# Order and form of the first loads, place of the filter copies, and number of product buffers in a fused spectral filter and feed-forward kernel

## The chip, the cores and the metric

The kernel runs on one core of a Trainium2 chip. The time is the device time of one launch in microseconds, the median of three runs. A core has TensorE (PE, matmul; PEld is its weight load), VectorE (DVE), ScalarE (ACT), GpSimd (POOL) and SyncE (SP), which works on queues of DMA transfers. Data lie in SBUF (128 partitions), matmul results in PSUM (8 banks), inputs and outputs in device memory.

## What is computed

```python
def _attn_ref(x, filt_r, filt_i):              # x: 8 x 3008 x 256 fp32
    X = np.fft.rfft(x, axis=1)                 # along the 3008 rows
    Y = X * (filt_r + 1j * filt_i)[None]       # a filter for each frequency and column
    return np.fft.irfft(Y, n=x.shape[1], axis=1).astype(np.float32)

def _moe_ref(x, w_in, w_out):                  # x: 24064 x 256, d_ff = 2048
    h = x @ w_in
    return (np.maximum(0.01 * h, h) @ w_out).astype(np.float32)
```

The second function takes the result of the first. The eight batches go through both, one after the other.

## The kernel before

The transform of 3008 = 94 x 32 is four stages of matmuls in fp16. Stage 1 (`s1`) transforms over 94 rows with `fwd1`, stage 2 (`s2`) over 32 with 24 matrices `f2_sb`, then the product with the filter, stage a (`sa`) and stage b (`sb`) go back. The result `yt` goes through the feed-forward part in 47 chunks of 512 tokens.

Between the stages the data have to change their place among the partitions. For the first batch VectorE does this with transposes (`t1`, `t2`), since nothing else is ready to run; batches 1 to 7 do it through device memory (`dz1`, `dz2`), beside the feed-forward part of the batch before. So the time falls into two parts: the first batch alone (its order of steps is the string `FIRST`), and everything after, in which TensorE does the feed-forward part with the later batches' stages between.

The loads at the start. GpSimd's queue casts fp32 to fp16 on the way; SyncE's queue [...] carries the constant matrices, which are fp16:

```python
    nc.sync.dma_start(small_sb[:], small_d.ap())               # fwd1, inv2 and others
    for i in (1, 0):
        nc.sync.dma_start(f2_sb[:, ts(i, NC // FP), :], f2_d.ap()[i])   # two thirds of stage 2's matrices
    first_parts = ((0, 10), (10, 10), (20, 8), (28, 4))
    for n0, nn in first_parts:
        x_load(0, n0, nn)                                      # batch 0, by GpSimd
    for hf in range(2):
        filt_load(0, filt_r, hf * DH, DH)                      # half of the columns; two transfers each
        filt_load(64, filt_i, hf * DH, DH)
        if hf == 0:
            nc.gpsimd.dma_start(f2_sb[:, ts(2, NC // FP), :], f2_d.ap()[2])
    nc.gpsimd.dma_start(w_in_sb[:], moe_w_in.rearrange("(dt p) c -> p dt c", p=P))
```

The steps of the first batch. `p` fills a PSUM bank, `e` empties it on ScalarE (A) or VectorE (D). `s2d` multiplies with the filter on VectorE straight out of PSUM; `s2a` copies to SBUF on ScalarE, and `s2m` multiplies there on GpSimd[...]. `warm` is matmuls on a tile of zeros whose result nobody uses:

```python
    spare = [scrp.tile([P, 4, DH], FP32, tag=f"p{i // 2 + 1}", name=f"spare{i}") for i in range(6)]

    def keep_warm(n):
        for _ in range(n):
            nc.tensor.matmul(po_ps..., idle[:, 0:P], idle[:], start=True, stop=True)
    def s1p(_, n0, n, b):                      # rows n0 to n0 + n into bank b
        ...
            nc.tensor.matmul(ps[:, ds(j, 2), :], fwd1[:N1], x_sb[:N1, ds(n0 + j, 2), :], start=True, stop=True)
    def s1e(_, n0, n, e):
        spread(big[0], n0, held.pop(("s1", n0)), engine[e])
    def t1(i):                                 # a quarter of the transposes after stage 1; t2 after stage a
        ...
        nc.vector.transpose(o[:, ts(i, E4)], a)
    def s2p(hf, c, n, i, b):                   # half hf of the columns, matrices c to c + n, part i, bank b
        ...
    def load_i1():                             # stage b's matrices
        nc.vector.memset(i1_sb[:, 0, 0:2], 0.0)
        nc.sync.dma_start(i1_sb[:], i1_d.ap())
    def load_x():                              # batch 1, and the output weights
        x_load(1, 0, N2 // 2)
        nc.gpsimd.dma_start(w_out_sb[:], moe_w_out.rearrange("(ct p) d -> p ct d", p=P))
        x_load(1, N2 // 2, N2 // 2)
```

Batches 1 to 7 take the product like this. Two buffers each of `p1`, `p2`, `p3`; the halves of `p2` change places by DMA (or, for every second group of batch 1, VectorE writes them in their new places):

```python
    scrp = ctx.enter_context(tc.tile_pool(name="scr", bufs=2))
    def s2_group(b, g):
        ...
            p1, p2, p3 = (scrp.tile([P, 2, D], FP32, tag=f"p{i}", ...) for i in (1, 2, 3))
            if b == 1 and g % 2 == EXG:
                nc.vector.tensor_tensor(p3[0:64], ps[64:P], fb[64:P], AL.mult)
                nc.vector.tensor_tensor(p3[64:P], ps[0:64], fb[0:64], AL.mult)
            else:
                nc.vector.tensor_tensor(p2[:], ps, fb, AL.mult)
                soon(AFTER[1], lambda: nc.sync.dma_start(p3[0:64], p2[64:P]))
                soon(AFTER[1], lambda: nc.sync.dma_start(p3[64:P], p2[0:64]))
            nc.vector.tensor_tensor(p1[:], ps, fa, AL.mult)
            ...  # later, on GpSimd: y1 = p1 + p3
```

For this they need the filter in another layout than the first batch, and VectorE makes it in six copies. `at(t, f)` puts `f` at a place `t` in the order in which instructions are issued; eight units are one chunk of the feed-forward part:

```python
    TWICE = (1.43, 1.84)
    for i in range(2):
        k1s = ts(i, NC // 2)
        for n, f in enumerate((
                lambda v=k1s: nc.vector.tensor_scalar(fb_sb[64:P, v], fa_sb[64:P, v], -1.0, None, AL.mult),
                lambda v=k1s: dve(fb_sb[0:64, v], fa_sb[64:P, v]),
                lambda v=k1s: dve(fa_sb[64:P, v], fa_sb[0:64, v]))):
            at(TWICE[0] + TWICE[1] * (3 * i + n), f)
```

Of the kernel before, what the change touches and what calls it, by code (L numbers as in the profile page):

```python
# [11 lines left out]
P = 128  # L12
FP16 = mybir.dt.float16
FP32 = mybir.dt.float32
# [5 lines left out]
N1, N2 = 94, 32  # L20
NC = 24
Q = 32
R1 = 96
FP = 3
# [51 lines left out]
def kernel(  # L76
# [9 lines left out]
    nc = tc.nc  # L86
    B, N, D = x.shape
# [16 lines left out]
    SUMS = (0.09, 1.59, 2.35, 4)  # L104
    REST = (5.37, 14.61, 8.86, 10.48, 23.53, 20.72)
    DUE = (3.52, 0.66)
    TWICE = (1.43, 1.84)
    F2T = 3.24
    LEAD = (3.85, 7.37)
    AFTER = (0.53, 0.8, 1.33, 3.17, 0.39, 0.52)  # L110
# [10 lines left out]
    f2_d = nc.inline_tensor(f2_np, name="fwd2_const")  # L121
    i1_d = nc.inline_tensor(i1_np, name="inv1_const")
# [5 lines left out]
    f2_sb = cpool.tile([P, NC, P], FP16, name="f2_sb")  # L128
    i1_sb = cpool.tile([P, N2, N1], FP16, name="i1_sb")
# [4 lines left out]
    w_out_sb = cpool.tile([P, NCT, D], FP16, name="w_out_sb")  # L134
    wt_sb = cpool.tile([P, 4, NCH, P], FP16, name="wt_sb")
    x_sb = cpool.tile([P, N2, D], FP16, name="x_sb")
    big = [cpool.tile([P, Q * D], FP16, name=f"big{i}") for i in range(3)]
# [1 line left out]

    gtp = ctx.enter_context(tc.tile_pool(name="gtp", bufs=2))  # L140
    drp = ctx.enter_context(tc.tile_pool(name="drp", bufs=1, space=bass.MemoryType.DRAM))
    scrp = ctx.enter_context(tc.tile_pool(name="scr", bufs=2))
    ypp = ctx.enter_context(tc.tile_pool(name="ypp", bufs=4))
    outp = ctx.enter_context(tc.tile_pool(name="outst", bufs=4))
    psp = ctx.enter_context(tc.tile_pool(name="psp", bufs=1, space=bass.MemoryType.PSUM))
# [18 lines left out]
    def at(time, f):  # L164
        clock["n"] += 1
        heapq.heappush(work, (time, clock["n"], f))
# [8 lines left out]
    def noted(what, f):  # L175
        f()
        issued.add(what)
# [10 lines left out]
    def x_load(b, n0=0, nn=N2, d0=0, dn=D):  # L188

        for lo, cnt in ((0, R1),) if b + 1 < B else ((0, 64), (64, N1 - 64)):  # L190
            nc.gpsimd.dma_start(
                x_sb[lo : lo + cnt, ds(n0, nn), ds(d0, dn)],
                bass.AP(tensor=x.tensor, offset=x.offset + (b * N + lo * N2 + n0) * D + d0,
                        ap=[[N2 * D, cnt], [D, nn], [1, dn]]))

    def filt_load(lo, src, d0, dn):

        for q, first, sgn in ((lo, 0, 1), (lo + Q, N1, -1)):
            nc.gpsimd.dma_start(
                fa_sb[q : q + Q, :, ds(d0, dn)],  # L200
                bass.AP(tensor=src.tensor, offset=src.offset + first * D + d0,
                        ap=[[N1 * D, N2 // 2], [sgn * NC * D, 2], [sgn * D, NC], [1, dn]]))


    nc.sync.dma_start(small_sb[:], small_d.ap())
    for i in (1, 0):
        nc.sync.dma_start(f2_sb[:, ts(i, NC // FP), :], f2_d.ap()[i])
    first_parts = ((0, 10), (10, 10), (20, 8), (28, 4))
    for n0, nn in first_parts:
        x_load(0, n0, nn)  # L210
    for hf in range(2):

        filt_load(0, filt_r, hf * DH, DH)
        filt_load(64, filt_i, hf * DH, DH)
        if hf == 0:
            nc.gpsimd.dma_start(f2_sb[:, ts(2, NC // FP), :], f2_d.ap()[2])
    nc.gpsimd.dma_start(w_in_sb[:], moe_w_in.rearrange("(dt p) c -> p dt c", p=P))
    idle = cpool.tile([P, CH], FP16, name="idle")
    nc.vector.memset(idle[:], 0.0)
# [136 lines left out]
    engine = {"A": act, "D": dve}  # L356
# [87 lines left out]
        sb_matmuls(ps, dt, h)  # L444
        quad_copy(h, dt, ps, copy)

    def load_i1():
        nc.vector.memset(i1_sb[:, 0, 0:2], 0.0)
        nc.sync.dma_start(i1_sb[:], i1_d.ap())

    def load_x():

        x_load(1, 0, N2 // 2)
        nc.gpsimd.dma_start(w_out_sb[:], moe_w_out.rearrange("(ct p) d -> p ct d", p=P))
        x_load(1, N2 // 2, N2 // 2)
        issued.add(("x", 1, 0))

    FIRST = """
        warm 18, s1p 0 0 2 b0, s1e 0 0 2 A, s1p 0 2 4 b3, s1p 0 6 4 b4, s1e 0 2 4 D, warm 4, s1p 0 16 4 b3,
        s1e 0 16 4 D, s1p 0 10 2 b1, s1e 0 6 4 A, s1p 0 12 4 b4, s1e 0 10 2 A, warm 2, s1p 0 24 2 b2,  # L460
        s1e 0 12 4 A, s1e 0 24 2 D, s1p 0 20 4 b3, s1e 0 20 4 A, s1p 0 26 2 b0, s1p 0 28 2 b1,
        s1p 0 30 2 b2, s1e 0 26 2 D, s1e 0 28 2 A, s1e 0 30 2 D, t1 1, t1 0, warm 14, s2p 0 0 4 0 b0,
        s2p 0 0 4 1 b1, s2p 0 16 4 0 b2, t1 2, t1 3, s2a 0 0 4 0, s2m 0 0 4 0, s2a 0 0 4 1, s2p 0 16 4 1 b0,
        s2p 0 8 8 0 b4, s2p 0 8 8 1 b3, s2a 0 16 4 0, s2m 0 16 4 0, s2a 0 16 4 1, s2m 0 16 4 1,
        s2p 0 4 4 0 b1, s2d 0 8 8 0, s2p 0 20 4 1 b2, s2d 0 8 8 1, i1, s2d 0 4 4 0, s2p 0 4 4 1 b0,
        s2p 1 8 8 0 b4, s2d 0 4 4 1, warm 1, s2p 1 8 8 1 b3, s2a 1 8 8 0, s2m 0 0 4 1, sap 0 8 b1,
        s2a 1 12 8 0, s2p 1 16 8 0 b4, s2d 0 20 4 1, sap 0 16 b0, s2m 1 12 8 0, x, s2a 1 8 8 1, s2m 1 8 8 1,
        s2d 1 16 8 0, sae 0 8 A, s2a 1 12 8 1, sae 0 16 A, s2p 0 20 4 0 b2, sap 0 4 b1, s2m 1 12 8 1,
        s2p 1 16 8 1 b3, sap 0 0 b0, s2p 1 0 8 1 b4, s2d 0 20 4 0, s2d 1 16 8 1, sae 0 4 A, s2m 1 8 8 0,
        sae 0 0 A, sap 0 20 b1, s2d 1 0 8 1, sap 0 12 b2, s2p 1 0 8 0 b3, sap 1 16 b0, sae 0 20 A,  # L470
        sae 0 12 A, sap 1 12 b1, s2d 1 0 8 0, sap 1 20 b2, t2 0, sap 1 8 b4, t2 1, sae 1 16 A, sap 1 4 b0,
        sap 1 0 b3, sae 1 12 A, warm 5, sbp 0 1 b1, sae 1 20 A, sae 1 8 A, sbp 0 4 b2, sae 1 4 A, sae 1 0 A,
        t2 3, sbp 0 5 b4, sbe 0 1 A, sbp 0 2 b0, t2 2, sbe 0 4 A, sbp 0 6 b3, sbe 0 5 A, sbp 0 7 b1,
        sbp 0 0 b2, sbp 0 3 b4, sbe 0 6 A, sbp 1 1 b3, sbe 0 0 D, sbe 0 2 A, sbp 1 0 b0, sbe 0 3 A,
        sbe 0 7 A, sbe 1 1 D, sbe 1 0 A
    """
    steps = dict(s1p=s1p, s1e=s1e, t1=t1, s2p=s2p, s2d=s2d, s2a=s2a, s2m=s2m, sap=sap, sae=sae, t2=t2,
                 sbp=sbp, sbe=sbe, i1=load_i1, x=load_x, warm=keep_warm)
    for step in FIRST.split(","):
        what, *args = step.split()  # L480
        steps[what](*(int(v) if v.isdigit() else v for v in args))
# [175 lines left out]
# [7 lines that stand above are left out]
    at(F2T, lambda: noted(("f2t",), lambda: nc.sync.dma_start(f2_sb[:], f2t_d.ap())))  # L664
    at(26, lambda: noted(("i1t",), lambda: nc.sync.dma_start(i1_sb[:K4], i1t_d.ap())))
    for b in range(1, B):
        z = 47 * (b - 4) if b > 4 else 0
        p = PLANS[min(b, 4) - 1]
# [18 lines left out]
    while queue:  # L687
        time, n, stage, b, g, f = heapq.heappop(queue)
# [62 lines left out]
```

## Time and profile before

| What | Value |
| --- | --- |
| time, median of 3 | 753.74 us (753.54 to 753.84) |
| span of the profiled run | 752.2 us |
| granted TensorE clock | 0.999 |
| busy: PE, DVE, ACT, POOL | 738.8, 499.3, 559.0, 163.6 us |
| first matmul of stage 1 | 8.02 us |
| VectorE's transposes after stage 1 | start at 14.68 us |
| first matmul of the feed-forward part | 36.23 us |

A line of the groups or the timeline of the profile names the line of the kernel, the engine, the operation, what it writes and reads, and how long it took; "[0.96 <-PE ph L388]" behind it says that the engine stood idle for 0.96 us before, and that the bank written at line 388 by TensorE released it. A line of the waits gives the engine that waited, for whom, the sum in microseconds, how often and the longest. Lines of the kernel before that matter here: 250 is stage 1 of batches 1 to 7 and 253 its copy out of PSUM, 299 stage 2, 308 and 311 the products, 314 GpSimd's sum, 321 stage a, 342 stage b, 379 and 425 the transposes of the first batch, 388 and 392 its stage 2, 396 its products, 406 and 419 ScalarE's copies, 502 the first matmul of the feed-forward part.

### The profile page before, as it was taken

The page shows a single profiled execution, that of the slowest core. Times are in us where ns is not written, and L with a number is a line of the kernel's source. Part 1 is how long each engine was busy: PE and PEld are TensorE (multiplying, and loading weights), DVE is VectorE, ACT ScalarE, POOL GpSimd, SP SyncE. Part 2 cuts the span into 40 slices and gives each one's busy share as a digit, 9 for nine tenths or more (in the row PEclk, how much of TensorE's full clock was granted, in tenths as well). Part 3 has the DMA queues.
Part 4 walks back from the last instruction along what each step waited for, and adds up shares of the span by engine and source line. Part 5 has one row for each costly group of instructions (what it writes and reads, how often), then busy time and mean ns, then how long its engine had stood idle before and what let it go on. Part 6 is the DMA issues. An engine that isn't in the chain of part 4 may idle for free.

```text
span 752.2 us, 19384 instructions
## 1 busy us (share of the span) xinstructions
PE 738.8 (98%) x8016; PEld 528.9 (70%) x8016; DVE 499.3 (66%) x683; ACT 559.0 (74%) x755; POOL 163.6 (22%) x169
## 2 busy tenths in 40 slices
PE   8999999999999999999999999999999999999997
PEld 3655667767777777877778777787777777777775
DVE  5886645777767776666676656776677576465565
ACT  3775797888878777787777787787777777777662
POOL 5503330342322311221133222212212210000000
PEclk9999999999999999999999999999999999999999
DMA  9986788887876557655676566544554333111011
GB/s 191 229 217 158 180 201 245 203 190 192 233 192 162 142 171 213 137 150 152 183 190 167 143 170 169 150 129 128 144 154 122 106 107 104 52 54 54 29 52 62
DMA packets 119688, 113.34 MB, mean 151 GB/s; under 512 B 16352, under 2 KB 92768, under 8 KB 119408
## 3 DMA queue, kind: packets, MB, share of 16 engines
q1 hardware_dynamic: 104447, 95.36, 42.7%
q0 software_dynamic: 14864, 16.49, 16.0%
q8 instruction: 62, 1.02, 0.6%
q10 hardware_dynamic: 289, 0.26, 0.1%
q14 instruction: 26, 0.21, 0.1%
HBM read 57.51 MB, written 50.33 MB: 143 GB/s over the span
## 4 chain that ended last, share of the span: by engine, by line
PE 91%; DMA 2%; DVE 2%; POOL 1%; ACT 0%; issue 0%; SPq 0%; DVEq 0%; ACTq 0%
PE ph L502 42%; PE po_ps L566 18%; PE pf L566 18%; PE pf L250 3%; PE pf L342 3%; PE pf L321 2%; PE pf L299 2%; PE po_ps L627 1%; PE pf L627 1%; DMA dz<-big 1%; DMA p_b_g<-p_b_g 1%; POOL prod L396 0%; DMA big<-dz 0%; POOL y_b_g L314 0%; DVE big L425 0%
## 5 line engine op out<-in xcount | busy, mean ns | idle before, releaser
L507 ACT ACTIVATE gt_c<-ph 128x1024 f16<-128x1024 f32 x376 | 385.4, 1025 | 134.8 <-PE ph L502 124.1
L502 PE MATMUL ph<-yt,w_in_sb 128*128 128x512 f16 (+7 forms) x1728 | 447.2, 351 | 0.5 <-DVE yt L332 0.5
L566 PEld LDWEIGHTS <-gt_c 128*128 128x128 f16 x2800 | 202.2, 98 | 91.1
L314 POOL TENSOR_TENSOR y_b_g<-p_b_g,p_b_g 128x512 f16<-128x512 f32 x84 | 115.4, 1374 | 418.8 <-DMA p_b_g<-p_b_g 245.4
L566 PEld LDWEIGHTS <-big 128*128 128x128 f16 x2128 | 151.3, 98 | 61.6 <-issue 0.2
L502 PEld LDWEIGHTS <-w_in_sb 128*128 128x128 f16 x1728 | 137.5, 98 | 20.9 <-issue 1.8
L308 DVE TENSOR_TENSOR p_b_g<-pf,fb_sb 128x512 f32<-128x512 f32 x78 | 53.6, 688 | 32.4 <-PE pf L299 17.3
L566 PE MATMUL po_ps<-wt_sb,gt_c 128*128 128x128 f16 x704 | 70.0, 219 | 0.0
L566 PE MATMUL pf<-wt_sb,gt_c 128*128 128x128 f16 x688 | 68.4, 219 | 0.0
L566 PE MATMUL pf<-w_out_sb,gt_c 128*128 128x128 f16 x720 | 67.9, 219 | 0.0
L566 PE MATMUL po_ps<-wt_sb,big 128*128 128x128 f16 x720 | 67.4, 219 | 0.0
L566 PE MATMUL pf<-wt_sb,big 128*128 128x128 f16 x704 | 67.2, 219 | 0.0
L253 ACT CAST big<-pf 128x512 f16<-128x512 f32 x100 | 58.3, 588 | 11.9 <-PE pf L250 10.5
L566 PE MATMUL po_ps<-w_out_sb,gt_c 128*128 128x128 f16 x688 | 66.0, 219 | 0.0
L332 ACT CAST yt<-pf 128x376 f16<-128x376 f32 x120 | 56.4, 473 | 12.2 <-PE pf L342 8.9
L311 DVE TENSOR_TENSOR p_b_g<-pf,fa_sb 128x512 f32<-128x512 f32 x84 | 57.2, 681 | 1.4 <-POOL y_b_g L314 1.3
L539 DVE TENSOR_TENSOR big<-gt_c 128x2048 f16<-128x2048 f16 (+1 forms) x46 | 57.9, 1259 | 0.1
L539 DVE TENSOR_TENSOR gt_c<-gt_c 128x2048 f16<-128x2048 f16 x43 | 56.1, 1305 | 1.0
L539 DVE TENSOR_TENSOR big<-big,gt_c 128x2048 f16<-128x2048 f16 (+1 forms) x45 | 53.9, 1197 | 0.1
L539 DVE TENSOR_TENSOR big<-gt_c,big 128x2048 f16<-128x2048 f16 (+1 forms) x45 | 53.8, 1197 | 0.0
L323 ACT CAST big<-pf 128x512 f16<-128x512 f32 x84 | 49.0, 584 | 5.8 <-PE pf L321 4.0
L250 PE MATMUL pf<-x_sb,small_sb 94*128 94x512 f16 x112 | 42.7, 381 | 0.8 <-DVE big L253 0.8
(85 smaller groups left out, 618.1 us busy)
## 6 DMA issues: line engine op xcount, KB each, us to landing
dz<-big SPq DMA_DIRECT2D x98, 256.0 KB
p_b_g<-p_b_g SPq DMA_DIRECT2D x156, 128.0 KB
out_dram<-ost_c_h SPq DMA_DIRECT2D x119, 128.0 KB
big<-dz SPq DMA_DIRECT2D x42, 256.0 KB
big<-dz SPq DMA_DIRECT2D x56, 192.0 KB
x_sb<-in_x_dram POOLq DMA_DIRECT2D x41, 192.0 KB, 4.5
x_sb<-in_x_dram POOLq DMA_DIRECT2D x2, 768.0 KB, 12.1
w_in_sb<-in_moe_w_in_dram POOLq DMA_DIRECT2D x1, 1024.0 KB, 12.9
```

The costliest lines, as they stand in the source:

```text
L250: nc.tensor.matmul(ps, fwd1[:N1], x_sb[:N1, ds(2 * g, 2), :], start=True, stop=True)
L253: copy(st[:, ds(2 * (g % 2), 2), :], ps)
L308: nc.vector.tensor_tensor(p2[:], ps, fb, AL.mult)
L311: nc.vector.tensor_tensor(p1[:], ps, fa, AL.mult)
L314: ("y", b, g), lambda: nc.gpsimd.tensor_tensor(y1[:], p1[:], p3[:], AL.add)))
L323: nc.scalar.copy(st2[h % 4][:, ds(2 * (g % 2), 2), :], ps)
L332: copy(yv, ps.rearrange("p c a -> p a c"))
L342: nc.tensor.matmul(ps[:, j, :], z2[h % 4][:K4, j, ts(dt, P)], i1_sb[:K4, 4 * h + j, :], start=True, stop=True)
L502: nc.tensor.matmul(ph[:, j, ds(t - ci * CH, e - t)], w_in_sb[:, dt, ts(ct, P)], yt[:, dt, ds(t % N, e - t)], start=(dt == 0), stop=(dt == ...
L507: nc.scalar.activation(gts[ci][:, ds(2 * g, 2), :], ph, AF.Lrelu)
L539: nc.vector.tensor_tensor(*(v[:, ds(c0, n)] for v in (o, i0, i1)), op)
L566: nc.tensor.matmul(po[:, t], a()[:, c, ts(t, P)], w[:, c, :], start=(c == 0), stop=(c == NCH - 1))
```

## The change

It has four parts. The first six of the 32 row groups of x come over SyncE's queue as fp32, into a part of a buffer that isn't used yet, and ScalarE and VectorE round them to fp16; they are meant to be there early. All other matrices go over GpSimd's queue, in the order in which the steps use them, and stage b's matrices are loaded there instead of in the middle of the products. The filter copies stand later, behind the copies out of PSUM that ScalarE does. The product buffers are three instead of two. The order of the first batch's steps is fitted to the new loads; its long string is shown up to the middle here.

```diff
-    TWICE = (1.43, 1.84)
+    TWICE = (2.2, 2.35)
...
-    scrp = ctx.enter_context(tc.tile_pool(name="scr", bufs=2))
+    scrp = ctx.enter_context(tc.tile_pool(name="scr", bufs=3))
...
+    EARLY = 6
+    x_early = big[1][:].bitcast(FP32)[:, : EARLY * D].rearrange("p (n d) -> p n d", n=EARLY)
     nc.sync.dma_start(small_sb[:], small_d.ap())
-    for i in (1, 0):
-        nc.sync.dma_start(f2_sb[:, ts(i, NC // FP), :], f2_d.ap()[i])
-    first_parts = ((0, 10), (10, 10), (20, 8), (28, 4))
-    for n0, nn in first_parts:
+    nc.sync.dma_start(x_early[:R1], bass.AP(tensor=x.tensor, offset=x.offset, ap=[[N2 * D, R1], [D, EARLY], [1, D]]))
+    for n0, nn in ((6, 10), (16, 10), (26, 6)):
         x_load(0, n0, nn)
+    for i in range(2):
+        nc.gpsimd.dma_start(f2_sb[:, ts(i, NC // FP), :], f2_d.ap()[i])
     for hf in range(2):
         ...
             nc.gpsimd.dma_start(f2_sb[:, ts(2, NC // FP), :], f2_d.ap()[2])
+    nc.gpsimd.dma_start(i1_sb[:], i1_d.ap())
     nc.gpsimd.dma_start(w_in_sb[:], moe_w_in.rearrange("(dt p) c -> p dt c", p=P))
...
-    def load_i1():
-        nc.vector.memset(i1_sb[:, 0, 0:2], 0.0)
-        nc.sync.dma_start(i1_sb[:], i1_d.ap())
-
-    def load_x():
-
-        x_load(1, 0, N2 // 2)
+    def load_x(half):
+        x_load(1, half * N2 // 2, N2 // 2)
+        issued.add(("x", 1, 0))
+
+    def load_w_out():
         nc.gpsimd.dma_start(w_out_sb[:], moe_w_out.rearrange("(ct p) d -> p ct d", p=P))
-        x_load(1, N2 // 2, N2 // 2)
-        issued.add(("x", 1, 0))
+
+    def round_x(n0, n, e):
+        engine[e](x_sb[:N1, ds(n0, n), :], x_early[:N1, ds(n0, n), :])
 
     FIRST = """
-        warm 18, s1p 0 0 2 b0, s1e 0 0 2 A, s1p 0 2 4 b3, s1p 0 6 4 b4, s1e 0 2 4 D, warm 4, s1p 0 16 4 b3,
-        s1e 0 16 4 D, s1p 0 10 2 b1, s1e 0 6 4 A, s1p 0 12 4 b4, s1e 0 10 2 A, warm 2, s1p 0 24 2 b2,
-        s1e 0 12 4 A, s1e 0 24 2 D, s1p 0 20 4 b3, s1e 0 20 4 A, s1p 0 26 2 b0, s1p 0 28 2 b1,
-        s1p 0 30 2 b2, s1e 0 26 2 D, s1e 0 28 2 A, s1e 0 30 2 D, t1 1, t1 0, warm 14, s2p 0 0 4 0 b0,
-        s2p 0 0 4 1 b1, s2p 0 16 4 0 b2, t1 2, t1 3, s2a 0 0 4 0, s2m 0 0 4 0, s2a 0 0 4 1, s2p 0 16 4 1 b0,
-        s2p 0 8 8 0 b4, s2p 0 8 8 1 b3, s2a 0 16 4 0, s2m 0 16 4 0, s2a 0 16 4 1, s2m 0 16 4 1,
...
+        xc 0 4 A, xc 4 2 D, warm 18, s1p 0 0 4 b3, s1p 0 4 2 b0, warm 3, s1p 0 14 2 b1, s1e 0 4 2 D,
+        s1e 0 0 4 A, s1p 0 10 4 b4, s1e 0 10 4 A, s1p 0 6 4 b3, s1e 0 14 2 D, warm 4, s1p 0 20 4 b4,
+        s1e 0 6 4 D, s1p 0 16 4 b3, s1e 0 16 4 A, s1p 0 26 2 b2, s1p 0 24 2 b0, s1e 0 24 2 A, s1e 0 20 4 D,
+        s1p 0 28 2 b1, s1p 0 30 2 b4, s1e 0 26 2 D, s1e 0 30 2 A, s1e 0 28 2 D, t1 0, t1 1, warm 14,
+        s2p 0 0 4 0 b3, s2p 0 0 4 1 b2, warm 2, s2p 0 8 4 1 b0, s2a 0 0 4 0, s2a 0 0 4 1, t1 3,
+        s2p 0 12 4 1 b4, t1 2, s2d 0 8 4 1, s2p 0 12 4 0 b1, s2p 0 16 8 0 b3, s2m 0 0 4 0, s2m 0 0 4 1,
...
+        x 0, s2m 1 16 8 0, sae 1 20 A, s2m 1 16 8 1, x 1, w_out, sae 1 12 A, sae 1 8 A, sap 1 16 b3,
...
     """
```

In both strings VectorE keeps ten products (six of eight matrices, four of four) and GpSimd eight, and the last steps are eight copies on ScalarE and two on VectorE.

More of the change, by code (lines that the diff above doesn't have):

```diff
@@ L464 @@
-        s2p 0 8 8 0 b4, s2p 0 8 8 1 b3, s2a 0 16 4 0, s2m 0 16 4 0, s2a 0 16 4 1, s2m 0 16 4 1,
[L465 to L473, printed above, removed]
@@ L474 @@
-        sbp 0 0 b2, sbp 0 3 b4, sbe 0 6 A, sbp 1 1 b3, sbe 0 0 D, sbe 0 2 A, sbp 1 0 b0, sbe 0 3 A,
-        sbe 0 7 A, sbe 1 1 D, sbe 1 0 A
+        xc 0 4 A, xc 4 2 D, warm 18, s1p 0 0 4 b3, s1p 0 4 2 b0, warm 3, s1p 0 14 2 b1, s1e 0 4 2 D,
+        s1e 0 0 4 A, s1p 0 10 4 b4, s1e 0 10 4 A, s1p 0 6 4 b3, s1e 0 14 2 D, warm 4, s1p 0 20 4 b4,
+        s1e 0 6 4 D, s1p 0 16 4 b3, s1e 0 16 4 A, s1p 0 26 2 b2, s1p 0 24 2 b0, s1e 0 24 2 A, s1e 0 20 4 D,
+        s1p 0 28 2 b1, s1p 0 30 2 b4, s1e 0 26 2 D, s1e 0 30 2 A, s1e 0 28 2 D, t1 0, t1 1, warm 14,
@@ new lines @@
+        s2p 0 0 4 0 b3, s2p 0 0 4 1 b2, warm 2, s2p 0 8 4 1 b0, s2a 0 0 4 0, s2a 0 0 4 1, t1 3,
+        s2p 0 12 4 1 b4, t1 2, s2d 0 8 4 1, s2p 0 12 4 0 b1, s2p 0 16 8 0 b3, s2m 0 0 4 0, s2m 0 0 4 1,
+        s2d 0 16 8 0, s2a 0 12 4 1, s2p 0 8 4 0 b2, s2p 1 16 8 0 b4, s2p 0 4 4 1 b0, s2a 0 12 4 0, s2d 0 8 4 0,
+        s2a 1 16 8 0, s2p 0 4 4 0 b1, s2p 1 16 8 1 b3, s2d 0 4 4 0, s2a 1 20 8 0, sap 0 8 b2, s2d 0 4 4 1,
+        s2a 1 16 8 1, s2a 1 20 8 1, s2m 0 12 4 0, s2p 0 16 8 1 b4, sap 0 0 b1, s2p 1 0 8 1 b3, s2m 0 12 4 1,
@@ new lines @@
+        sap 0 12 b0, s2m 1 20 8 0, sae 0 8 A, s2d 0 16 8 1, sae 0 0 A, s2p 1 8 8 1 b4, sap 0 4 b2, s2d 1 0 8 1,
+        sap 0 16 b1, sae 0 12 A, s2p 1 8 8 0 b3, sap 0 20 b0, s2d 1 8 8 1, s2m 1 20 8 1, sae 0 4 A,
+        s2d 1 8 8 0, s2p 1 0 8 0 b4, sae 0 16 A, sap 1 20 b2, s2d 1 0 8 0, sap 1 12 b1, sae 0 20 A, sap 1 8 b0,
+        x 0, s2m 1 16 8 0, sae 1 20 A, s2m 1 16 8 1, x 1, w_out, sae 1 12 A, sae 1 8 A, sap 1 16 b3,
+        sae 1 16 A, sap 1 4 b2, t2 1, sae 1 4 A, sap 1 0 b4, t2 0, sae 1 0 A, warm 4, sbp 0 1 b1, sbp 0 4 b0,
@@ L476 @@
+        sbp 0 0 b3, sbp 0 3 b2, t2 3, sbe 0 1 A, sbe 0 4 A, sbe 0 0 A, sbp 0 2 b4, sbp 0 7 b1, sbp 0 6 b0,
+        t2 2, sbe 0 2 A, sbe 0 7 A, sbp 0 5 b3, sbp 1 0 b4, sbp 1 1 b1, sbe 0 6 A, sbe 0 5 A, sbe 1 1 A,
+        sbe 0 3 D, sbe 1 0 D
     """
     steps = dict(s1p=s1p, s1e=s1e, t1=t1, s2p=s2p, s2d=s2d, s2a=s2a, s2m=s2m, sap=sap, sae=sae, t2=t2,
-                 sbp=sbp, sbe=sbe, i1=load_i1, x=load_x, warm=keep_warm)
+                 sbp=sbp, sbe=sbe, x=load_x, w_out=load_w_out, xc=round_x, warm=keep_warm)
```

## The prediction

> **What bounds the kernel now.** I read the busy table first, then the stages, then what TensorE waits for, then the order of time inside the one stage that is not TensorE's.
>
> The busy table of the page:
>
> ```profile
> PE 738.8 (98%) x8016; PEld 528.9 (70%) x8016; DVE 499.3 (66%) x683; ACT 559.0 (74%) x755; POOL 163.6 (22%) x169
> ```
>
> TensorE is busy 98%, but "warm" matmuls on a zero tile count as busy too. So the stages matter (columns: window, sum, busy time of PE, PEld, DVE, ACT, POOL, granted clock, DMA share, GB/s):
>
> ```profile
> 0.00:8.00 8.00, 6.81 (x18) 2.50 (x19) 1.19 (x3) 1.49 (x2) 5.21 (x12) 1.00 0.81 176
> 8.00:14.70 6.70, 6.36 (x29) 2.55 (x28) 4.45 (x6) 4.82 (x6) 3.15 (x5) 1.00 1.34 194
> 14.70:36.20 21.50, 19.05 (x264) 11.96 (x263) 19.71 (x21) 13.88 (x28) 12.36 (x13) 1.00 1.35 225
> 36.20:116.00 79.80, 75.96 (x556) 47.08 (x556) 49.26 (x75) 57.97 (x77) 20.60 (x23) 1.00 0.78 193
> 116.00:752.00 636.00, 630.63 (x7156) 464.78 (x7153) 424.72 (x579) 480.88 (x643) 122.31 (x117) 1.00 0.54 142
> ```
>
> From 116 us on TensorE has no gap (the 5.4 us missing there are the tail after the last matmul), and the change touches none of its work. What can move lies before 116: the first batch (0 to 36.2 us), and 3.84 us of gaps in 36.2 to 116. From 14.7 to 36.2 VectorE is busy 19.71 of 21.50: that stage is VectorE's. The waits of TensorE name the gaps (total, times, longest):
>
> ```profile
> PE pf L342 <- DMA big<-dz: 1.2, 1, 1.2
> ...
> PE pf L388 <- DMA f_sb<-fwd_const: 1.1, 1, 1.1
> PE pf L299 <- DVE p_b_g L311: 1.0, 1, 1.0
> PE pf L250 <- DVE big L253: 0.8, 2, 0.5
> PE pf L321 <- DVE p_b_g L311: 0.8, 1, 0.8
> PE ph L502 <- DVE yt L332: 0.5, 1, 0.5
> ```
>
> And VectorE and GpSimd in order of time (start, length):
>
> ```profile
> 14.68 4.62 DVE L379 STREAM_TRANSPOSE big<-big 128x1024 f32<-128x1024 f32 x4
> ...
> 20.27 2.36 DVE L396 TENSOR_TENSOR prod<-ph,fa_sb 128x1024 f16<-128x1024 f32 x2 [0.96 <-PE ph L388]
> ...
> 25.20 1.18 POOL L454 DMA_DIRECT2D w_out_sb<-in_moe_w_out_dram  x1
> ...
> 26.91 3.39 POOL L396 TENSOR_TENSOR prod<-spare,fa_sb 128x512 f16<-128x512 f32 x3
> ...
> 29.73 2.36 DVE L425 STREAM_TRANSPOSE big<-big 128x1024 f32<-128x1024 f32 x2
> ...
> 32.64 2.37 DVE L425 STREAM_TRANSPOSE big<-big 128x1024 f32<-128x1024 f32 x2 [0.55 <-ACT big L419]
> ```
>
> The reader is to see two holes in VectorE's chain: 0.96 us before the first product, because TensorE stood before the last third of the stage-2 matrix (landed at 18.9 us), and 0.55 us before the last two transposes, because ScalarE waited for GpSimd's last product, which ended at 26.91 + 3.39 = 30.30, behind 2.3 us of issuing transfers (24.60 to 26.90).
>
> **What the Trainium skill says.** "DMA: Bandwidth & Descriptors", section "Issuing engines are not separate DMA queues": transfers issued by any engine run on the same 16 DMA engines and interleave. The trace agrees: in the first 10 us SyncE's queue takes 22.0% and GpSimd's 63.2% of the 16 engines. So moving the matrices from one queue to the other brings no bandwidth; it only changes who goes first. "VectorE: DVE Perf Modes", section "The perf-mode tier table": a tensor_tensor with an operand in PSUM has no faster mode than one element a cycle. The product of 128x1024 takes 1220 ns here, near 1024 over the page's 0.96 GHz = 1.07 us (an estimate from that page) plus a fixed part. So the ten products VectorE keeps cannot shrink; only holes between them can go. "TensorE: Matmul & The Clock Gate", section "What's actually happening": TensorE runs at half clock until it has been busy some microseconds. The trace agrees: the first warm matmuls follow each other every 0.43 us, later ones every 0.216. So the 18 warm matmuls ahead of the first real one (1.19 to 8.18 us, with the overlap of the last) must stay, and both versions have 18.
>
> **The change part by part.**
>
> *First rows in fp32.* The rows 0 to 5 come over SyncE's queue and are rounded by ScalarE (four rows, about 1 us, estimated from its 1.02 us for 128x1024) and VectorE (two). They replace two thirds of the stage-2 matrix (512 KB) there, with 96 x 1536 x 4 B = 576 KB, so GpSimd's first transfer meets about as much traffic as before and lands near 8.0 us. The first matmul now starts at 8.02 us; the 18 warm matmuls hold it there in the new version too. After that GpSimd carries 26 rows in place of 32. A ten-row part took 10.41 - 8.05 = 2.4 us from landing to landing, so six rows are worth 1.4 us: the last part should land near 12 us, not 13.05. But stage 1 is then limited by emptying PSUM. VectorE has two copies of 1.23 us and four of 0.67 (5.1 us, before 4.47), ScalarE three of 1.05 and two of 0.6 (4.4 us). Walking the new order by hand: VectorE starts at 8.8, waits for TensorE some 0.4 us, ends near 14.4; ScalarE ends at 14.2 to 14.6. Transposes start at **14.5**, before 14.68: a gain of 0.2, not of 1.
>
> *Matrices in the order of use.* Two thirds of the stage-2 matrix go behind x, the last third stays behind half of the filter. That third lands near 18.9 as before, but the new order works on the first two thirds meanwhile (columns 0, 8, 12) and comes to column 16 only after 19 us. VectorE then goes from the transposes (14.5 + 4.62 = 19.1) straight into products: the hole of 0.96 is gone. Its products are the same, six of 128x1024 and four of 128x512. They filled 20.27 to 29.80 = 9.53 us; now 19.1 to **28.7**.
>
> *Transfers of batch 1 later on GpSimd.* Of the three issues only the first x half stays between products (0.6 us). GpSimd's eight products take 8 x 1.16 = 9.3 us. Started at 18.2 as before, with some 0.6 us of waiting, they end near 28.7, before 30.30. So the last transposes wait for VectorE itself: two pairs of 2.36, 28.7 to **33.5**, before 35.01. Then follow the last matmuls, the copies and the first matmul of the feed-forward part, 1.2 us after the transposes now (36.23). But ScalarE has eight copies of about 0.43 us there (3.5 us) after its last stage-a copy near 31, which ends near 35. I take **34.9 to 35.1** for the start, a gain of **1.2 us**.
>
> *Filter copies.* Six copies of 0.95 us on VectorE stand between copies of batch 1's stage 1, and TensorE waits for those twice (0.33 at 40.63, 0.51 at 43.25). Put where ScalarE empties the bank, most of the 0.8 should go: **0.6 us**. The last one moves to just ahead of batch 1's first products, where VectorE has 2.84 us and 1.44 us idle now, so it fits.
>
> *Three product buffers.* VectorE waits 0.22 and 0.67 us for a product buffer that GpSimd still reads (its sum waits for the swap through DMA, 4.48 us at 66.84). The second of these passes on to TensorE as the 0.8 us at L321. A third buffer takes both away: **0.7 us**. The 1.0 us at L299 is VectorE's own chain of 0.69 us products (66.42 to 68.53, without a hole), and the 1.2 us at L342 is a chain of transfers through memory; both stay.
>
> Sum: 1.2 + 0.6 + 0.7 = 2.5 us, or 0.3%. 753.74 - 2.5 = 751.2; a tenth back for what doesn't fit: **751.3 us**.
>
> **The rivals.** First, *PSUM emptying eats the start and ScalarE the end*: the prologue's gain is only the hole of 0.96 less what ScalarE adds. For it: both engines have over 4.4 us of copies in a stage of 6.5 us. Then the prologue gives 0.5 and the whole about 752.0. Second, *GpSimd's queue becomes the wait*: it holds more transfers ahead of its first product, and each issue there waits for an older landing (it now waits 1.83, 1.99 and 1.01 us so). With two more parts of the matrix and the inverse matrix in it, the feed-forward weights go out near 17.5 us in place of 15.41; if it is 19 or later, the products start late and the last transposes wait again for GpSimd: 753.5 to 754.5. Against it: TensorE and ScalarE don't have the first operand before 18 us anyway. Third, *batch 1 or the output weights come too late*: the second half of x and w_out now queue behind the inverse matrix (752 KB) and w_in. From the 12.9 us that w_in took and 12 to 13 for each next one, overlapping, I estimate 37 us for x and 43 for w_out; they are used from about 41 and 46. If w_out misses, TensorE waits 1 to 2 us and the gain is gone: 753 to 754. Fourth, *the gaps after 36 us move instead of closing*, as a bank freed earlier only brings TensorE to the next slow transfer: 752.5.
>
> **Range and chances.** All parts as worked out give 751.2; with the second hole of VectorE also replaced by a faster start, 749.8; the rivals give 752 to 754.5. I set the range at 749.7 to 753.2. The lever is 36 + 4 us out of 752, so 2% (15 us) either way is nearly out of reach: 0.005 and 0.005.
>
> **What would show it.** Right: first matmul still near 8.0; VectorE's first transpose at 14.2 to 14.8; its first product without a hole, near 19.1; the last transpose's end near 33.5; the first feed-forward matmul at 34.7 to 35.3; the waits of L250 for VectorE under 0.3; the wait of L321 gone, L299 and L342 still there. Wrong: a TensorE wait for the filter, the matrix, w_in or w_out; GpSimd's first product after 19; or a first matmul well before or after 8.0, which would say that the rows' landing and not the warm matmuls set it.

## The result and the profile after

The changed kernel takes **749.97 us** (749.38 to 751.10), the kernel before 753.64 beside it: a ratio of 0.9953, 95% interval 0.9936 to 0.9970. The gain is 3.7 us, where 2.4 were predicted; it lies within the stated range, near its fast end. The profiled run took 749.61 us, 4.4 less than the profiled run of before (754.03).

The busy table of the changed kernel, and its stage from 36.2 to 116 us (columns as before):

```profile
PE 737.9 (99%) x8017; PEld 528.6 (71%) x8017; DVE 499.9 (67%) x684; ACT 559.1 (75%) x755; POOL 167.5 (22%) x171
```

```profile
36.20:116.00 79.80, 78.24 (x609) 49.89 (x608) 51.27 (x77) 59.91 (x82) 20.92 (x23) 1.00 0.84 205
```

TensorE's busy time is nearly that of before (738.8); its gaps in that stage fell from 3.84 to 1.56 us. What is left of its waits:

```profile
PE pf L303 <- DVE p_b_g L315: 0.9, 1, 0.9
PE pf L254 <- ACT big L257: 0.6, 1, 0.6
PE ph L392 <- issue: 0.5, 1, 0.5
PE ph L505 <- ACT yt L336: 0.2, 1, 0.2
PE pf L437 <- DVE big L429: 0.2, 1, 0.2
```

Lines 303, 254, 392 and 505 are 299, 250, 388 and 502 of the kernel before, and below 325 and 346 are its 321 (stage a) and 342 (stage b). The waits at stage a (0.8) and stage b (1.2) are gone, so is the one for the stage-2 matrix (1.1). At line 254 two waits for VectorE have become one for ScalarE. The first batch in order of time:

```profile
6.26 1.04 ACT L459 CAST x_sb<-big 94x1024 f16<-94x1024 f32 x1 [4.02 <-DMA big<-in_x_dram]
7.36 0.59 PE L374 MATMUL ph<-x_sb,small_sb 94*128 94x512 f16 x2
...
14.01 4.63 DVE L383 STREAM_TRANSPOSE big<-big 128x1024 f32<-128x1024 f32 x4 [0.29 <-ACT big L283]
...
18.56 0.65 DVE L400 TENSOR_TENSOR prod<-pf,fa_sb 128x512 f16<-128x512 f32 x1
...
25.18 2.28 POOL L400 TENSOR_TENSOR prod<-spare,fa_sb 128x512 f16<-128x512 f32 x2
...
28.23 4.71 DVE L429 STREAM_TRANSPOSE big<-big 128x1024 f32<-128x1024 f32 x4
...
33.91 1.19 PE L505 MATMUL ph<-yt,w_in_sb 128*128 128x512 f16 x4 [0.21 <-ACT yt L336]
```

In this profile VectorE's chain has no holes: transposes 14.01 to 18.6, products from 18.56, four transposes in one piece to 32.94. GpSimd's last product ends at 27.46 (25.18 + 2.28) and holds nobody. The feed-forward part starts at 33.91 us, before at 36.23. That is 2.3 us; the 2.1 us that make up the 4.4 come after it.

### The profile page after: what moved, and what is told of

Same layout as the page of the kernel before. It is cut to its first block, busy times and chain, and to the rows that moved or that the text cites. A ratio compares the mean times of both kernels' runs of the same rounds, so it can differ in the third digit from the quotient of the medians.

```text
span 747.8 us, 19408 instructions
## 1 busy us (share of the span) xinstructions
PE 737.9 (99%) x8017; PEld 528.6 (71%) x8017; DVE 499.9 (67%) x684; ACT 559.1 (75%) x755; POOL 167.5 (22%) x171
## 4 chain that ended last, share of the span: by engine, by line
PE 93%; DMA 2%; DVE 2%; ACT 1%; issue 0%; POOL 0%; SPq 0%; DVEq 0%; POOLq 0%
PE ph L505 42%; PE po_ps L569 18%; PE pf L569 18%; PE pf L254 3%; PE pf L346 3%; PE pf L303 2%; PE pf L325 2%; DMA p_b_g<-p_b_g 2%; PE pf L630 1%; PE po_ps L630 1%; DMA big<-in_x_dram 1%; PE po_ps L368 1%; POOL y_b_g L318 0%; ACT yt L336 0%; PE ph L396 0%
## 5 line engine op out<-in xcount | busy, mean ns | idle before, releaser
L318 POOL TENSOR_TENSOR y_b_g<-p_b_g,p_b_g 128x512 f16<-128x512 f32 x84 | 117.8, 1403 | 415.0 <-DMA p_b_g<-p_b_g 255.2
L542 DVE TENSOR_TENSOR big<-gt_c,big 128x2048 f16<-128x2048 f16 (+1 forms) x45 | 55.3, 1228 | 0.0
L542 DVE TENSOR_TENSOR gt_c<-gt_c 128x2048 f16<-128x2048 f16 x43 | 54.6, 1269 | 1.0
```

Of the source, the lines that this page charges most:

```text
L318: ("y", b, g), lambda: nc.gpsimd.tensor_tensor(y1[:], p1[:], p3[:], AL.add)))
L542: nc.vector.tensor_tensor(*(v[:, ds(c0, n)] for v in (o, i0, i1)), op)
```

## The experiments

The kernels of each set of four ran on one chip beside the kernel before; set 1 ran on another chip than sets 2 and 3. "Start" is the first matmul of the feed-forward part in the kernel's profiled run.

| kernel | median us | ratio to before (95% interval) | start us |
| --- | --- | --- | --- |
| set 1: two buffers | 751.22 | 0.9982 (0.9973 to 0.9990) | 34.08 |
| copies early | 750.92 | 0.9970 (0.9958 to 0.9981) | 34.41 |
| before, with buffers and copies | 752.25 | 0.9985 (0.9978 to 0.9991) | 35.10 |
| 15 warm matmuls | 749.54 | 0.9958 (0.9945 to 0.9971) | 34.30 |
| set 2: the changed kernel | 749.93 | 0.9957 (0.9945 to 0.9969) | 34.34 |
| matrices by SyncE | 750.90 | 0.9972 (0.9964 to 0.9980) | 35.64 |
| all rows cast | 749.98 | 0.9959 (0.9948 to 0.9971) | 34.11 |
| issues early | 751.75 | 0.9977 (0.9967 to 0.9986) | 36.00 |
| set 3: issues last | 750.35 | 0.9967 (0.9955 to 0.9978) | 34.02 |
| first batch only | 751.47 | 0.9979 (0.9968 to 0.9989) | 34.69 |
| the kernel before | 753.12 | 0.9997 (0.9987 to 1.0006) | 35.51 |
| before, issues late | 753.36 | 0.9998 (0.9988 to 1.0009) | 35.49 |

The kernel before had medians of 753.30, 753.35 and 753.49 in the three sets, but single runs of it lie from 751.6 to 756.6. A single profile is therefore one draw: I read mechanisms from profiles and sizes from medians. The ratios give somewhat other sizes: against the changed kernel's 0.9957 two buffers lose 1.9 us by the ratio and 1.3 by the median, issues early 1.5 and 1.8, copies early 1.0 by both. The sizes below are good to about half a microsecond.

**Two buffers.** One line of the changed kernel:

```diff
-    scrp = ctx.enter_context(tc.tile_pool(name="scr", bufs=3))
+    scrp = ctx.enter_context(tc.tile_pool(name="scr", bufs=2))
```

> The changed kernel with two product buffers again. Theory A (the buffers close only the wait of stage a): the waits of VectorE for GpSimd's sum (0.2 and 0.7 us) and TensorE's 0.8 us at stage a come back, the 1.2 us wait of stage b for its transfer stays away; 750.7. Theory B (the earlier sums also brought the stage-b transfer forward): both waits come back, 751.9. Theory C (the buffers do nothing for the end): 750.0. In all of them the first feed-forward matmul stays at 33.9.

The waits of TensorE that are new against the changed kernel's page:

```profile
PE pf L325 <- DVE p_b_g L315: 0.7, 1, 0.7
...
PE pf L346 <- DVE p_b_g L315: 0.4, 1, 0.4
...
PE pf L346 <- DMA big<-dz: 0.2, 1, 0.2
```

The wait at stage a (L325) is back, as A has it; theory B's return of the long transfer wait did not come, and C is out. The median lost 1.3 us against 749.93, 0.5 more than A gave. The rest is not shown to come from the buffers: the 0.4 at stage b (at 133 us) is absent in the other profiles with two buffers and stands with 0.3 in one with three, issues early.

**Filter copies early.**

```diff
-    TWICE = (2.2, 2.35)
+    TWICE = (1.43, 1.84)
```

> The changed kernel with the filter copies at their old places. Theory A: TensorE waits for VectorE's stage-1 copies again, 0.8 us in sum in place of the 0.6 us that it now waits for ScalarE; the move was worth only 0.2 to 0.3, so 750.2. Theory B (a late copy of the old order was also what held the stage-b transfer): the 1.2 us wait comes back, 751.4. First feed-forward matmul at 33.9 in both.

```profile
PE pf L254 <- DVE big L257: 0.9, 2, 0.5
...
PE po_ps L569 <- DVE big L612: 0.4, 1, 0.4
```

The two waits for VectorE are back at 0.9, and the one of 0.6 for ScalarE is gone, as A has it. But the median lost 1.0, not 0.3; the profile adds 0.4 for a later VectorE sum (at 173 us; issues last, whose copies are late, has it too) and 0.2 at stage b. The intervals of this kernel and the changed one overlap (0.9958 to 0.9981, 0.9945 to 0.9969), so the size stays rough.

**The kernel before with three buffers and late copies.**

```diff
-    TWICE = (1.43, 1.84)
+    TWICE = (2.2, 2.35)
...
-    scrp = ctx.enter_context(tc.tile_pool(name="scr", bufs=2))
+    scrp = ctx.enter_context(tc.tile_pool(name="scr", bufs=3))
```

> The kernel before with three product buffers and the later filter copies, its first batch untouched. Theory A (all of the gain after 36 us comes from these two): first feed-forward matmul at 36.2, no wait at stage a or stage b, 751.6. Theory B (the stage-b wait went because of the new loads): the wait of 1.2 us stays, 752.7.

Its first product on VectorE, and the waits of TensorE after 36 us:

```profile
18.90 2.35 DVE L396 TENSOR_TENSOR prod<-ph,fa_sb 128x1024 f16<-128x1024 f32 x2
```

```profile
PE pf L342 <- DMA big<-dz: 1.2, 1, 1.2
...
PE pf L299 <- DVE p_b_g L311: 1.0, 1, 1.0
PE pf L250 <- ACT big L253: 0.6, 1, 0.6
```

Stage a's wait is gone, stage b's 1.2 us stands. Theory A falls, B is right: the stage-b wait goes with the loads and order of the first batch. The two parts alone are worth 1.05 us (753.30 less 752.25), which is about what the waits lost: 0.8 at stage a, 0.2 at stage 1.

The profile also shows something about the hole of 0.96 us. The first batch is untouched here, and yet VectorE goes from the transposes (14.36 + 4.63 = 18.99) straight into its products, and TensorE has no wait for the last third of the matrix. In the four profiles with the old first batch the hole was 0.96, 0.68, 0.77 and none; in ten with the new one it was absent but for one (0.67, in first batch only). So in both it depends on when that third lands.

**Fifteen warm matmuls.**

```diff
-        xc 0 4 A, xc 4 2 D, warm 18, s1p ...
+        xc 0 4 A, xc 4 2 D, warm 15, s1p ...
```

> The changed kernel with 15 warm matmuls ahead of the first real one in place of 18. Theory A: TensorE's clock goes to full rate at another moment in each run, somewhere from 5.4 us (seen in the changed kernel's profile) to 7.1 us (seen in that of the kernel before), and where it is late the 18 warm matmuls last to 8.2 us and hold the first real one back; this makes the spread of 749.4 to 751.1. With 15 they end by 7.4 us in the late case too, so the runs lie within 0.6 us and the median is 749.5. Theory B: the spread comes from the transfers later on; spread and median stay. Theory C: with 15 the clock turns later, during stage 1; 750.5 and a first transpose after 14.4.

The first real matmul came at 7.19 us after waiting 0.68 for ScalarE's rounding, and the runs still spread from 749.13 to 751.12. So with 15 it is the rounding that holds the start, and the narrower spread of theory A did not come: the clock's turn alone does not make it (five runs). C did not come either; B remains, with its transfers: this profile had 0.8 us of waiting at stage b, the changed kernel's two profiles none; that this makes the spread is not shown. The median is 749.54, with an interval that can't be told from the changed kernel's.

**The changed kernel again.** No edit.

> The changed kernel itself, beside the three others on one chip, since the runs of one version were seen to differ by up to 2 us. Theory A (what differs is when transfers land): first real matmul between 7.0 and 7.9, set by the end of the rounding; stage b's wait for its transfer anywhere from 0 to 1.2; 749.4 to 751.2, median 750.2. Theory B (what differs is the clock's turn to full rate): the first real matmul follows the warm ones without a wait.

The runs were 749.57 to 750.13. The first real matmul came at 7.31, behind the warm ones without a wait, as B has it; in four other profiles of versions with the early rows and 18 warm matmuls it waited 0.2 to 0.6 us for the rounding, as A has it, so the two end near each other and either can be last. The 18 warm matmuls took from 5.4 to 7.0 us in thirteen profiles, since the clock turned to full rate earlier or later: their distance fell from 0.43 to 0.216 us at 4.1 us in the earliest and at 7.1 in the latest. Stage b's wait was absent. This second profile shows a hole that the first did not have:

```profile
17.72 4.54 POOL L400 TENSOR_TENSOR prod<-spare,fa_sb 128x512 f16<-128x512 f32 x4 [0.46 <-DMA fa_sb<-in_filt_i_dram]
23.86 2.29 POOL L400 TENSOR_TENSOR prod<-spare,fa_sb 128x512 f16<-128x512 f32 x2 [1.60 <-DMA fa_sb<-in_filt_i_dram]
26.10 0.60 POOL L191 DMA_DIRECT2D x_sb<-in_x_dram  x1
26.71 2.28 POOL L400 TENSOR_TENSOR prod<-spare,fa_sb 128x512 f16<-128x512 f32 x2
```

```profile
31.11 2.37 DVE L429 STREAM_TRANSPOSE big<-big 128x1024 f32<-128x1024 f32 x2 [0.39 <-ACT big L423]
```

The second half of the filter landed near 23.8 us, GpSimd stood 1.60 us for it, and its last product at 28.99 held the transposes by 0.39. This is no exception: in four more of the ten profiles with the new first batch (two buffers, 15 warm matmuls, all rows cast, issues last) GpSimd stood 1.7 to 1.9 us for the same half. In three of these its last product again held the transposes by 0.4. The landing of the filter is the next thing that can bind.

**Two thirds of stage 2's matrices by SyncE again.**

```diff
     for i in range(2):
-        nc.gpsimd.dma_start(f2_sb[:, ts(i, NC // FP), :], f2_d.ap()[i])
+        nc.sync.dma_start(f2_sb[:, ts(i, NC // FP), :], f2_d.ap()[i])
```

> The changed kernel with the first two thirds of stage 2's matrices on SyncE's queue again, behind the early rows. Theory A (order of use matters, because they share the DMA engines with x): the second and third part of x land about 1 us later, the first transpose starts near 15.0 in place of 14.0, the filter lands 1.3 us earlier; 751.0. Theory B (only VectorE and ScalarE limit stage 1): first transpose at 14.0 to 14.3, time as the changed kernel, 750.0.

```profile
PE pf L374 <- DMA x_sb<-in_x_dram: 1.1, 1, 1.1
PE pf L325 <- POOL y_b_g L318: 1.1, 1, 1.1
...
PE ph L374 <- ACT x_sb L459: 0.6, 1, 0.6
...
PE ph L374 <- DMA x_sb<-in_x_dram: 0.3, 1, 0.3
```

TensorE waits for rows in stage 1, the transposes start at 15.71 and the median is 750.90: theory A, with the loss of 1.0 us that it gives. All 15 runs (750.35 and more) lie above the five of the changed kernel beside them (750.13 and less). The profiled run itself took 752.46, above the median; the wait at L325, at 214 us, is part of that.

**All rows cast on GpSimd's queue.**

```diff
-    nc.sync.dma_start(x_early[:R1], ...)
-    for n0, nn in ((6, 10), (16, 10), (26, 6)):
+    for n0, nn in ((0, 6), (6, 10), (16, 10), (26, 6)):
         x_load(0, n0, nn)
...
-        xc 0 4 A, xc 4 2 D, warm 18, s1p ...
+        warm 18, s1p ...
```

> The changed kernel with the first six rows cast on GpSimd's queue in place of fp32 on SyncE's, and so no rounding. Theory A (the purpose of the change: SyncE's queue starts earlier and so the rows come earlier): they land near 7.0, the other parts 1.2 us later than now; first transpose near 14.8; 751.0. Theory B (the engines read the same fp32 bytes either way, and what SyncE's queue gains the rounding takes back): rows land near 6.3, first matmul held by the warm ones at 7.3 or later, the last part of x lands at 12.4; first transpose within 0.4 of the changed kernel's; 750.0.

```profile
7.13 0.60 PE L373 MATMUL ph<-x_sb,small_sb 94*128 94x512 f16 x2
```

First matmul at 7.13, behind the warm ones, transposes at 13.79, median 749.98 against 749.93: theory B. **The rows in fp32, the part that the change begins with, are worth nothing that the runs can show.** The trace shows why: a packet that casts 6144 B of fp32 to 3072 B takes 248 ns, a plain packet of 6144 B on SyncE's queue 234 ns in the quickest quarter and 259 to 332 in the medians of six profiles. At this size the cast costs nothing, so the six rows land no earlier: their last packet ended at 5.15 us in the changed kernel and at 5.23 here. And ScalarE's 1.04 us of rounding stands behind the fp32 path.

**GpSimd's issues early.**

```diff
-        ... s2m 1 20 8 0, sae 0 8 A, ...
+        ... s2m 1 20 8 0, x 0, w_out, x 1, sae 0 8 A, ...
-        x 0, s2m 1 16 8 0, sae 1 20 A, s2m 1 16 8 1, x 1, w_out, sae 1 12 A, ...
+        s2m 1 16 8 0, sae 1 20 A, s2m 1 16 8 1, sae 1 12 A, ...
```

> The changed kernel with GpSimd issuing batch 1's rows and the output weights between its fifth and sixth product, as before the change. Theory A: GpSimd's last product ends 1.7 us later, near 29.6, the last two transposes wait about 0.6 us again, and the feed-forward part starts 0.6 to 0.9 us later; 750.9. Theory B (ScalarE's last copies set the end anyway): the same time, 750.1.

```profile
27.25 3.40 POOL L400 TENSOR_TENSOR prod<-spare,fa_sb 128x512 f16<-128x512 f32 x3
```

```profile
32.75 2.37 DVE L429 STREAM_TRANSPOSE big<-big 128x1024 f32<-128x1024 f32 x2 [2.04 <-ACT big L423]
```

GpSimd issues for 2.3 us and its last product ends at 27.25 + 3.40 = 30.65; VectorE has a hole of 2.04 us, the feed-forward part starts at 36.00 and the median is 751.75. Theory A, and twice its size: 1.8 us by the median. Against the changed kernel's second profile the last product ends 1.66 us later and the feed-forward part starts 1.66 later.

**Issues last**, a candidate for a faster version.

```diff
-        x 0, s2m 1 16 8 0, sae 1 20 A, s2m 1 16 8 1, x 1, w_out, ...
+        s2m 1 16 8 0, sae 1 20 A, s2m 1 16 8 1, x 0, x 1, w_out, ...
```

> The changed kernel with all three late issues of GpSimd (both halves of batch 1's rows, the output weights) behind its last product; a candidate for a version that beats both. Theory A (GpSimd's last product still holds the last two transposes, by the 0.4 us seen in the second profile of the changed kernel): its last product ends 0.6 us earlier, the transposes run without a hole, feed-forward part at 33.9, median 749.5. Theory B (batch 1's rows then come too late): TensorE waits for the rows, 750.5.

```profile
PE po_ps L630 <- DMA w_out_sb<-in_moe_w_out_dram: 3.0, 1, 3.0
```

The hole is gone (transposes 28.34 to 33.05, start at 34.02), as A has it, but the output weights now sometimes miss their use: 3.0 us in this profile, a run of 755.56, and three of 22 runs are above 754. The wait costs more than its 3.0 us: after it the granted clock is 0.50 for 3.4 us (clock, DMA share and GB/s are the last three columns):

```profile
50.20:53.60 3.40, 3.40 (x21) 1.74 (x19) 0.83 (x2) 1.42 (x2) 0.00 (x0) 0.50 1.11 331
```

I estimate that at 1.7 us, half of the 3.4. No other profile shows such a dip between its first turn to full rate and its end; their longest wait of TensorE after that is 1.6 us. The median is 750.35, no better than the changed kernel's. B was right that something comes late, but it was the weights, not the rows.

**First batch only.** Two buffers and early copies in the changed kernel, the two one-line edits above together.

> The changed kernel with two product buffers and the filter copies at their old places, so that only the loads and the order of the first batch are changed. Theory A (the two parts add): 749.93 and 1.3 for the buffers and 1.0 for the copies, 752.2; waits at stage a 0.8, of stage 1 for VectorE 0.9, stage b under 0.5. Theory B (the stage-b wait of 1.2 needs the old first batch and the old buffers together): 751.5. Theory C (the old buffers and copies overlap): 751.2.

751.47: theory B's figure, but not its mechanism, since the stage-b wait stood with the new buffers too. The waits are those of line 303 (1.0), 254 for VectorE (0.9) and 325 (0.8), and in the first batch 0.5 for the last third of stage 2's matrix; stage b has none. The edits cost 1.3 and 1.0 singly, 1.5 together: they overlap, as theory C has it, as far as such sizes can show it. The new first batch alone is worth 753.49 - 751.47 = 2.0 us (1.6 by the ratio).

**The kernel before again.** No edit.

> The kernel before once more, for a second profile of it. Theory A (its stage-b wait belongs to its order of loads): the wait of stage b for its transfer is 1.0 to 1.4 again, and the last write ahead of it takes over 6 us again. Theory B (chance): the wait is under 0.6. In both: feed-forward part at 35.0 to 36.3, depending on when the last third of stage 2's matrices lands.

```profile
101.52 0.36 SPq L325 DMA_DIRECT2D dz<-big  x1
104.47 0.94 SPq L325 DMA_DIRECT2D dz<-big  x1
111.15 1.75 SPq L269 DMA_DIRECT2D big<-dz  x4
```

The wait of stage b was 0.9 us, near A's figure: the last write is issued at 104.47 and the reads follow 6.7 us later. The changed kernel, in its first profile:

```profile
101.86 0.36 SPq L329 DMA_DIRECT2D dz<-big  x1
107.18 1.74 SPq L273 DMA_DIRECT2D big<-dz  x4
```

Here it is 5.3 us, and the issue itself takes 0.36 in place of 0.94. This holds throughout: in four profiles with the old first batch the issue took 0.82 to 0.94 us, the reads followed after 6.5 to 6.9, and stage b waited 0.9 to 1.6; in ten with the new one it took 0.36 to 0.38, after 5.1 to 5.9, and stage b waited 0 to 0.8. So the stage-b wait goes with the first batch, 60 us and more earlier. The matrices on SyncE's queue and the rows in fp32 don't carry it: with one of these taken back (two thirds of stage 2's matrices by SyncE, all rows cast) the wait was none and 0.3. The place of stage b's matrices and the order of the steps were not taken back singly.

What is different at the end of the write can be seen in the two microseconds before the reads, in the first profile of the kernel before and then of the changed one (DMA share and GB/s are the last two columns):

```profile
109.97:110.97 1.00, 1.00 (x12) 0.69 (x11) 0.42 (x1) 1.00 (x2) 0.00 (x0) 1.00 0.33 98
110.97:111.97 1.00, 1.00 (x13) 0.72 (x12) 0.00 (x0) 0.86 (x2) 0.00 (x0) 1.00 0.07 22
```

```profile
105.18:106.18 1.00, 1.00 (x12) 0.67 (x10) 0.59 (x1) 1.00 (x2) 0.00 (x0) 1.00 1.10 330
106.18:107.18 1.00, 1.00 (x12) 0.64 (x11) 0.40 (x1) 1.00 (x3) 0.00 (x0) 1.00 0.67 201
```

A share of 0.07, where all 16 DMA engines together show 1.10, is about what one engine gives (an estimate from these two numbers): it seems that at the end the reads wait for a few packets on one engine while the others are idle. Taken in halves of a microsecond, the share stays at or under 0.8 for the last 2.0 us in all four profiles with the old first batch, and for 0.5 to 1.5 in the ten with the new one. What makes the write end so unevenly there isn't settled.

**The kernel before with its issues late.**

```diff
-        ... s2m 1 12 8 0, x, s2a 1 8 8 1, ...
+        ... s2m 1 12 8 0, s2a 1 8 8 1, ...
-        ... s2m 1 8 8 0, sae 0 0 A, ...
+        ... s2m 1 8 8 0, x, sae 0 0 A, ...
```

> The kernel before with the three issues of GpSimd (batch 1's rows, the output weights) behind its last product instead of ahead of the last three; nothing else changed. Theory A (the hole before the last transposes is GpSimd's issuing): its last product ends 2.3 us earlier, the hole of 0.55 to 0.8 is gone, feed-forward part 0.5 to 0.8 earlier, 752.7. Theory B (batch 1's rows or the weights then come late and TensorE waits): 753.5 or more.

```profile
29.47 4.81 DVE L425 STREAM_TRANSPOSE big<-big 128x1024 f32<-128x1024 f32 x4
```

```profile
PE pf L250 <- DMA x_sb<-in_x_dram: 0.7, 1, 0.7
```

The hole closes, as A has it, and batch 1's second half of rows, which stands behind the weights here, comes 0.7 us late, as B has it. The median is 753.36: nothing gained. The changed kernel issues the rows ahead of the weights, one half of them early, and its profiles show no wait for rows or weights there.

## Why the prediction was right, and where not

**Right:** the time and its range, with the measured time near the fast end; that the gain lies ahead of 116 us (the changed kernel's two profiles have no wait of TensorE after that; some of other versions have 0.3 to 1.1 us at 133 to 214 us); that the hole of 0.96 us before the products goes, though it can be absent in the kernel before and come back in the new order; that VectorE's chain sets the first batch's end; and that a third buffer takes the 0.8 us at stage a. It gave 0.7 for that, and undone the wait came back with 0.7 and 0.8; the median of two buffers lost 1.3, and the rest of that is not explained.

**The step that failed: "the 1.2 us at L342 is a chain of transfers through memory; both stay".** The wait at L299 stayed, that at L342 went, in every version with the new first batch shrunk or absent. This is the larger part of what the sum missed: 0.9 to 1.2 us that it did not count. The chain of transfers is there as read, but its length was not fixed: from the last write's issue to the reads it took 5.3 us, not 6.7, with a shorter tail of low DMA share at the write's end. Why the new first batch brings that stays open.

**The first batch, 1.2 us, was of the right size for the typical run, in part by luck.** The two second profiles give 35.51 - 34.34 = 1.17; the two first ones 36.23 - 33.91 = 2.32, since the kernel before drew a late start there and the changed kernel an early one. Taking 1.2 for the start and 0.9 for stage b's wait gives 2.1, against 1.6 to 2.0 measured for the first batch alone. The two ends of the difference were both too late. I had read one profile of before as if it were the kernel; its 36.23 was 0.7 later than the next. And the new start, given as 34.9 to 35.1 behind ScalarE's copies, came at 33.91 and 34.34, ahead of the last of those copies (34.24 and 34.74).

**The first matmul near 8.0, held there by the warm ones, was wrong by 0.7.** The warm ones ended at 6.7 to 7.6 us in the profiles of the new versions, since the clock turned sooner than in the one profile I had read, and the first real one came at 7.0 to 8.0, behind them or behind the rounding. The transposes began at 14.0 for it, not at 14.5. The prediction took a first matmul well before 8.0 as a sign that the rows' landing sets it; here it came early mostly because the warm ones ended early, as in the second profile of the kernel before (7.37). Nor must there be 18 of them: with 15 the median was 749.54.

**Filter copies, 0.6:** the waits for VectorE did go (0.8 to none), but one of 0.6 for ScalarE took their place, as the fourth rival had it. Undone in the changed kernel the copies cost 1.0, undone together with the buffers only 0.2 more than the buffers alone (1.5 and 1.3); the size stays open between these. The waits alone give 0.2 to 0.3 (0.8 or 0.9 less 0.6).

**The rivals.** The first, PSUM's emptying at the start and ScalarE at the end, did not win: the transposes came 0.3 to 0.7 us earlier and the feed-forward part 1.2. The second, GpSimd's queue as the wait, did not win: the weights for the first feed-forward matmul went out at 16.3 to 16.6 us and its first product ran at 17.6 to 17.7. But it was near: the filter's second half often lands late, and three issues in the wrong place cost 1.8 us. The third, late output weights, is real only when they are put last, and then costs more than the 1 to 2 us given: 3.0 of waiting and the clock's dip.

## What to carry to other kernels

When an engine both computes on the critical path and issues transfers, look at where the issues stand in its order: 2.3 us of issuing between the products cost 1.5 to 1.8 us here, and putting them all last made the weights late. Before moving a load to another queue or saving a cast, compare packet durations and landings in the trace: the six rows landed at 5.15 us as fp32 and at 5.23 with the cast, while taking the matrices out of their order of use cost 1.0 us. Where a transfer has to land before another may start, look at its last microseconds too: here a share of 0.07 pointed to a few packets that the reads waited for. Take a second profile of the kernel before: a start that moves by 0.7 us between two profiles is as large as the parts that one tries to predict.

## What was not expected of the hardware

A transfer that casts fp32 to fp16 took as long per packet as a plain one of the same source bytes, for long packets (248 ns for 6144 B in and 3072 B out, 234 ns and more for 6144 B plain). For short ones it took longer: 41 ns for 512 B in and 256 B out, 27 ns for plain packets of 512 B, which here write to device memory.

TensorE's clock turned to full rate at another moment in each run, 2.9 to 6.0 us after the first warm matmul: the same 18 matmuls took 5.4 to 7.0 us. After a wait of 3.0 us it was granted at one half for 3.4 us.

The issue of one transfer on SyncE's queue took 0.82 to 0.94 us in the versions with the old first batch and 0.36 to 0.38 in those with the new one, over 60 us after it. In the old versions the write of 256 KB behind that issue ended with 2 us in which the DMA share fell to about 0.1, as if one or two of the 16 engines were left to work; in the new ones that tail took 0.5 to 1.5 us.
